# Casts moved into the DMA, fillers re-sized and casts spread in a fused sparse-attention and ELU-MLP kernel

## The chip, the cores and the metric

One core of one Trainium2 chip. The metric is the device time of one launch in microseconds (us). The kernel before takes 348.42 us, the median of three runs (348.39 to 350.0). All runs use one core, so a run counts as slow when it is over 1.5% above the fastest of the same kernel, and ratios use the other runs only.

## The reference, cut to what matters

```python
# q, k, v: (8 batches, 8 heads, 576, 64) float32
scores = (1/8) * q @ k.T
mask_local   = (rel >= 0) & (rel < 32)                    # heads 0 to 3
mask_strided = (rel >= 0) & (pos_k % 32 == pos_q % 32)    # heads 4 to 7
attn = softmax(where(mask, scores, -1e9)) @ v
x = attn.transpose(0, 2, 1, 3).reshape(4608, 512)
h = x @ w_in                                              # 512 -> 2048
g = where(h > 0, h, exp(min(h, 0)) - 1)
out = g @ w_out                                           # 2048 -> 512, float32
```

The matmuls run in bf16. Attention of one batch feeds 576 tokens to the two MLP layers, which are most of the work.

## The kernel before

Attention of batch 0 runs alone at the start (0 to 31 us). Layer one of its tokens follows, then batch 1 between pieces of layer two, and from about 75 us a loop mixes attention of batches 2 to 7 with the MLP. In the profiles PE is TensorE and PEld its weight loads, DVE is VectorE, ACT is ScalarE, POOL is GpSimd and SP is SyncE. `hpw` and `hps` are results of layer one (four and two blocks wide), `ops` of layer two, `g` is the ELU's output, and `so`, or `s_ps` and `o_ps`, are the sums and products that a tail takes up. A load lands when its data has arrived. In the program's names a piece `T` transposes q and k on TensorE, `S` makes scores, exp and the masked product `pm`, `M` multiplies by ones and v, `E` is the tail (ln, exp, product into `xT`), `X` is `M` and `E` together, `f` and a digit are filler matmuls that keep TensorE's clock up, and `2` is a quarter of a layer-two tile. In the list of batch 0, `c` is the second k cast, `m` the strided mask and `v` the v casts. Pieces are numbered by head pair and half: 0 to 3 are local, 4 to 7 strided.

The parts that the argument touches, cut (`# ...`):

```python
w_in_sb = const([128, KC, d_ff], BF16, "w_in_sb")        # one tile, two loads into it
for i in range(2):
    nc.gpsimd.dma_start(out=w_in_sb[:, :, i * 1024:(i + 1) * 1024],
                        in_=w_in_v[:, :, i * 1024:(i + 1) * 1024])
# ...
def cast_q(eng, a): ...      # ql32 (float32) -> qlb (bf16), on a chosen engine
def cast_k(eng, a): ...      # kl32 -> klb
def cast_v(eng, b, a): ...   # vl32 -> vlx[b % 2]
# ... batch 0
for it in ("f4 S0 S1 c f4 T1 m S2 f4 T2 S3 f4 S4 T3 f4 S5 f4 S6 M4 f2 S7 f2 E4 M5 f2 E5 M6 f2 E6 "
           "v M7 f2 E7 M0 f2 E0 M1 f2 E1 M2 f2 E2 M3 f8 E3").split():
    n = int(it[1]) if len(it) > 1 else 0                 # one digit only
    # ...
# ... batch 1, beside layer two of batch 0
for it in ("2 S4 2 S5 2 2 X4 2 S6 X5 2 S7 2 X6 2 X7 v "
           "a 2 2 T0 2 S0 S1 2 T1 B0 2 S2 B1 E0 2 S3 E1 B2 2 B3 E2 2 t E3 x").split():
    # "a" casts q on DVE, k on ACT and GpSimd, v on GpSimd;
    # "t" transposes the strided heads of batch 2; "B" is M in another buffer
    # ...
# ... layer two, at the end of a tile
if part == 3:
    nc.scalar.copy(o_sb, ops)                            # ACT; traced as osb<-ops
    store(j * SUB + kk * 128, o_sb)
# ... in the loop
def casts2():                # batch 2: k, q, k, q and then v, v, all on GpSimd
    ...
at(2, casts2)
```

The softmax here doesn't subtract the row's maximum and nothing guards it: scores larger than these inputs give would overflow.

## Time and profile before

| view | number |
|---|---|
| median of three runs | 348.42 us |
| the profiled run | 350.58 us, span 348.9 us, mean granted clock 0.966 |
| TensorE (PE) busy | 93% of the span |
| fillers in the trace | 74: 26 ahead of all, 48 in batch 0 |
| first layer-one group that runs in full | at 30.61 us |

The profiled run was 2 us longer than the median, and its clock lower than in most runs (0.966; the median of 96 later runs of this kernel is 0.980). A difference of two traces therefore overstates the gain by about 2 us, and what follows says where that matters.

The summary of the chain of waits, by engine, from the page of the kernel before:

```profile
PE 68%; ACT 12%; DVE 11%; DMA 4%; issue 3%; SPq 1%; ACTq 0%; DVEq 0%
```

TensorE is two thirds of it and DMA only 4%. The start of layer one in the timeline of PE. Columns: start and length in us, engine, line of the kernel, operation, what it writes from what, sizes, count; in brackets the idle time before and what ended it:

```profile
30.61 1.80 PE L393 MATMUL hpw<-xT,w_in_sb 128*128 128x256 bf16 x15 [0.26 <-DVE xT L282]
32.25 1.91 PE L367 MATMUL hps<-xT,w_in_sb 128*128 128x256 bf16 x16
```

Layer one waits for `xT`, the attention output of batch 0, for 0.26 us. The line says nothing of the weights, which had landed by then. By the trace of the loads the two halves of `w_in` were issued at 6.9 and 7.7 us and took 17.0 and 21.8 us, so the second landed at 29.5, only 1.1 us before.

### The profile page before, as it was taken

The page shows a single profiled execution, that of the slowest core. Times are in us where ns is not written, and L with a number is a line of the kernel's source. Part 1 is how long each engine was busy: PE and PEld are TensorE (multiplying, and loading weights), DVE is VectorE, ACT ScalarE, POOL GpSimd, SP SyncE. Part 2 cuts the span into 40 slices and gives each one's busy share as a digit, 9 for nine tenths or more (in the row PEclk, how much of TensorE's full clock was granted, in tenths as well). Part 3 has the DMA queues.
Part 4 walks back from the last instruction along what each step waited for, and adds up shares of the span by engine and source line. Part 5 has one row for each costly group of instructions (what it writes and reads, how often), then busy time and mean ns, then how long its engine had stood idle before and what let it go on. Part 6 is the DMA issues. An engine that isn't in the chain of part 4 may idle for free.

```text
span 348.9 us, 7582 instructions
## 1 busy us (share of the span) xinstructions
PE 323.0 (93%) x2926; PEld 222.9 (64%) x2926; DVE 247.1 (71%) x479; ACT 221.0 (63%) x426; POOL 109.2 (31%) x125
## 2 busy tenths in 40 slices
PE   7799898776989999999899999999999999999995
PEld 5557864354656666677566766666777766777762
DVE  4532994457767788889887897789888776766660
ACT  3466757654667777777677766777777776444441
POOL 8076712656257242615306351635000000000000
PEclk9658999996999999999999999999999999999999
DMA  8999998988649982999159975994193101111111
GB/s 161 187 201 204 218 165 134 202 159 178 111 86 139 197 176 56 135 195 203 41 85 133 210 172 103 169 216 114 30 150 72 38 24 34 49 30 32 43 49 60
DMA packets 49739, 43.26 MB, mean 124 GB/s; under 512 B 32808, under 2 KB 39720, under 8 KB 49704
## 3 DMA queue, kind: packets, MB, share of 16 engines
q0 software_dynamic: 15600, 25.77, 42.9%
q1 hardware_dynamic: 32780, 16.42, 23.6%
q10 hardware_dynamic: 1324, 0.59, 0.9%
q8 instruction: 23, 0.38, 0.5%
q14 instruction: 12, 0.10, 0.1%
HBM read 38.21 MB, written 9.44 MB: 137 GB/s over the span
## 4 chain that ended last, share of the span: by engine, by line
PE 68%; ACT 12%; DVE 11%; DMA 4%; issue 3%; SPq 1%; ACTq 0%; DVEq 0%
PE ops L426 28%; PE hps L367 27%; PE sc L258 4%; DVE he L382 3%; ACT he L375 3%; DVE g L383 2%; DMA kl<-in_k_dram 2%; ACT osb L431 2%; PE idle L436 2%; DMA ksT<-ks 2%; PE ox L310 1%; ACT ln L314 1%; ACT ln L313 1%; PE tp L233 1%; PE hpw L393 1%
## 5 line engine op out<-in xcount | busy, mean ns | idle before, releaser
L426 PE MATMUL ops<-w_out_sb,g 128*128 128x512 bf16 x576 | 146.9, 380 | 3.6 <-ACT osb L431 3.6
L367 PE MATMUL hps<-xT,w_in_sb 128*128 128x256 bf16 x1088 | 143.1, 275 | 2.3 <-DVE xT L282 1.4
L367 PEld LDWEIGHTS <-w_in_sb 128*128 128x128 bf16 x1088 | 116.1, 114 | 22.4 <-issue 2.8
L375 ACT ACTIVATE he<-hps 128x512 f32<-128x512 f32 x136 | 80.7, 595 | 64.1 <-PE hps L367 62.8
L383 DVE TENSOR_TENSOR g<-he,hps 128x512 bf16<-128x512 bf16 x130 | 89.4, 688 | 14.3 <-PE hps L367 1.0
L382 DVE TENSOR_SCALAR he<-he 128x512 bf16<-128x512 f32 x130 | 63.4, 488 | 25.2 <-ACT he L375 24.2
L426 PEld LDWEIGHTS <-g 128*128 128x128 bf16 x576 | 52.0, 98 | 44.5 <-issue 5.3
L261 ACT ACTIVATE e<-sc 128x576 bf16<-128x576 f32 (+1 forms) x64 | 41.0, 647 | 18.7 <-PE sc L258 18.6
L431 ACT COPY osb<-ops 128x512 f32<-128x512 f32 x36 | 21.0, 583 | 10.4 <-PE ops L426 9.3
L282 DVE TENSOR_TENSOR xT<-ox,rc 64x288 bf16<-64x288 f32 x40 | 18.2, 454 | 7.1 <-ACT rc L316 6.3
L278 DVE TENSOR_TENSOR xT<-ox,rc 64x288 bf16<-64x288 f32 x40 | 18.1, 454 | 6.3 <-ACT rc L316 5.7
L111 POOL DMA_DIRECT2D qs<-in_q_dram x8 | 6.5, 816 | 44.8 <-DMA qsT<-qs 33.8
L269 DVE TENSOR_TENSOR pm<-e,mask_l 128x576 bf16<-128x576 bf16 x32 | 15.5, 496 | 6.7 <-ACT e L261 6.5
L313 ACT ACTIVATE ln<-ox 64x288 f32<-64x288 f32 x40 | 16.3, 408 | 5.8 <-PE ox L310 4.9
L263 DVE TENSOR_TENSOR pm<-e,mask_s 72x576 bf16<-72x576 bf16 x32 | 15.9, 513 | 4.9 <-ACT e L261 4.9
L316 ACT ACTIVATE rc<-ln 128x288 f32<-128x288 f32 x40 | 17.8, 444 | 1.3
L132 POOL COPY vsx<-vs 72x1024 bf16<-72x1024 bf16 x10 | 10.7, 1095 | 25.0 <-DMA vs<-in_v_dram 25.0
L436 PE MATMUL idle<-warm 128*128 128x256 bf16 x74 | 16.1, 367 | 1.3 <-DVE warm L155 1.3
L126 POOL CAST vlx<-vl 128x768 bf16<-128x768 f32 x15 | 13.0, 890 | 12.5 <-DMA vl<-in_v_dram 11.5
L120 POOL CAST klb<-kl 96x768 bf16<-96x768 f32 x13 | 11.5, 884 | 16.0 <-DMA kl<-in_k_dram 10.0
L314 ACT ACTIVATE ln<-ox 64x288 f32<-64x288 f32 x40 | 16.1, 403 | 0.5
L117 POOL CAST qlb<-ql 72x1024 bf16<-72x1024 f32 x12 | 12.9, 1076 | 7.2 <-DMA ql<-in_q_dram 7.2
(86 smaller groups left out, 266.4 us busy)
## 6 DMA issues: line engine op xcount, KB each, us to landing
vl<-in_v_dram POOLq DMA_DIRECT2D x8, 576.0 KB, 17.2
out_dram<-osb SPq DMA_DIRECT2D x32, 144.0 KB
kl<-in_k_dram POOLq DMA_DIRECT2D x7, 576.0 KB, 14.1
ql<-in_q_dram POOLq DMA_DIRECT2D x7, 576.0 KB, 15.2
qs<-in_q_dram POOLq DMA_DIRECT2D x8, 288.0 KB, 6.7
ks<-in_k_dram POOLq DMA_DIRECT2D x8, 288.0 KB, 9.1
vs<-in_v_dram POOLq DMA_DIRECT2D x8, 288.0 KB, 10.4
w_in_sb<-in_moe_w_in_dram POOLq DMA_DIRECT2D x2, 1024.0 KB, 19.4
```

Of the source, the lines that this page charges most:

```text
L261: nc.scalar.activation(e[0:R], sc[0:R, :, 0:W], ACT.Exp, scale=scale)
L278: nc.vector.tensor_mul(xs[:, u * W:(u + 1) * W], o[pr], rc[pr])
L282: nc.vector.tensor_mul(dst, o[pr].rearrange(pat, b=3, s=NS), rc[pr].rearrange(pat, b=3, s=NS))
L313: nc.scalar.activation(ln[lo], o[0][hi], ACT.Ln)
L314: nc.scalar.activation(ln[hi], o[1][lo], ACT.Ln)
L367: nc.tensor.matmul(hps[:, mm], lhsT=w_in_sb[:, c, (m // 4) * 512:(m // 4 + 1) * 512].rearrange("c (p mm) -> c mm p", mm=4)[:, m % 4], rhs= ...
L375: nc.scalar.activation(e, hps, ACT.Exp)
L382: eng.tensor_scalar(e1, e, scalar1=1.0, scalar2=1.0, op0=ALU.min, op1=ALU.subtract)
L383: nc.vector.tensor_tensor(gt, e1, hps, op=ALU.max)
L426: nc.tensor.matmul(ops, lhsT=g[:, m, kk * 128:(kk + 1) * 128], rhs=w_out_sb[:, m, :], start=(m == 0), stop=(m == MC - 1))
L431: nc.scalar.copy(o_sb, ops)
L436: nc.tensor.matmul(ps, lhsT=warm[:, 0:128], rhs=warm[:, 0:ps.shape[-1]], start=True, stop=True, skip_group_check=True)
```

## The change

Its intent: take casts off the engines in the stretches where TensorE has holes. In the compute part the kernel after lies 25 lines further down, so L367, L382 and L393 become L392, L407 and L418. In its list of batch 0, `X3` is not `M` and `E` but `T3` with a wider PSUM buffer. The core of the diff, cut:

```diff
+    def load_ql16(b):   # cast in the DMA, straight into the tile that is read
+        nc.gpsimd.dma_start(out=qld[0:RS], in_=q[b, 0:HG].rearrange(...))
+    def load_kl16(b): ...      # one per head, into klb
+    def load_vl16(b): ...      # two per head, into vlx
@@ transposes of local q, batches 1 and 2: two halves of 64 columns each
+                if type(x) is list:
+                    for z in range(2):
+                        nc.tensor.transpose(o[z * D:(z + 1) * D], x[z], identity[0:n, 0:n])
@@ batch 0
+    cast_k(nc.vector, 1)                    # was on ACT
-    for it in ("f4 S0 S1 c f4 T1 m S2 f4 T2 S3 f4 S4 T3 f4 S5 f4 S6 M4 f2 S7 f2 E4 M5 f2 E5 M6 f2 E6 "
-               "v M7 f2 E7 M0 f2 E0 M1 f2 E1 M2 f2 E2 M3 f8 E3").split():
+    for it in ("f7 S0 S1 f6 T1 f6 S2 S3 m f10 T2 f6 S4 S5 f3 X3 f3 S6 f3 S7 M4 f3 E4 M5 f3 E5 M6 f3 E6 "
+               "v M7 f3 E7 M0 f3 E0 M1 f3 E1 M2 f3 E2 M3 f10 E3").split():
         n = int(it[1]) if len(it) > 1 else 0
@@ batch 1
+    nc.gpsimd.memset(qlb[64:RP], 0.0)       # was behind the loads
     load_kl(1, nc.gpsimd)
-    load_ql(1, nc.gpsimd)
+    load_ql16(1)
     load_vl(1, nc.gpsimd)
-    nc.gpsimd.memset(qlb[64:RP], 0.0)
     # ... four memsets of vlx and vsx stay here, one small one joins them
     load_str(2, ks, k)
+    load_vl16(2)
-               "a 2 2 T0 2 S0 S1 2 T1 B0 2 S2 B1 E0 2 S3 E1 B2 2 B3 E2 2 t E3 x").split():
+               "a 2 T0 2 S0 S1 2 T1 k B0 2 E0 S2 2 B1 S3 E1 2 B2 E2 2 B3 t 2 E3 x").split():
-            cast_q(nc.vector, 0)
-            cast_q(nc.vector, 1)
+        elif it == "k":
+            load_kl16(2); load_ql16(2); load_kl(3, ...); load_ql(3, ...); load_vl(3, ...)
@@ loop
-    at(2, casts2)
-        ld, sp, ca, tr = (9, 3, 4, 3) if b == 3 else (9, 6, 5, 3)
+        ld, sp, ca, tr = (9, 3, 5, 3) if b == 3 else (9, 6, 5, 3)
-        at(st - ca, lambda b=b: casts(b))
+        for i, f in enumerate(casts(b)):    # order k, k, q, q, v, v
+            at(st - ca + .5 * i, f)
```

More of the change, by code (lines that the diff above doesn't have):

```diff
@@ L76 @@
     qlb = const([RP, 2, NS, 2 * D], BF16, "qlb")
+    qld = qlb.rearrange("p a s c -> p (a s c)").rearrange("p (h c) -> p h c", h=HG)
     klb = const([LQ, 2, LB, 2 * D], BF16, "klb")
@@ L108, in load_vl, with load_kl16, load_vl16 @@
         eng.dma_start(out=t[0:PRE, 1:], in_=x[LQ - PRE:, 0:HG * LB - 1, :])
+    def load_ql16(b):
+        nc.gpsimd.dma_start(out=qld[0:RS], in_=q[b, 0:HG].rearrange("h (p s) d -> p h (s d)", s=NS))
+    def load_kl16(b):
+        for h in range(HG):
+            nc.gpsimd.dma_start(
+                out=klb[:, h // 2, :, (h % 2) * D:(h % 2 + 1) * D],
+                in_=k[b, h].rearrange("(t p) d -> p t d", p=LQ))
+    def load_vl16(b):
+        for h in range(HG):
+            x = v[b, h].rearrange("(t p) d -> p t d", p=LQ)
+            t = vlx[b % 2][:, h // 2, :, 2 * (h % 2) * D:(2 * (h % 2) + 1) * D]
+            nc.gpsimd.dma_start(out=t[PRE:128], in_=x)
+            nc.gpsimd.dma_start(out=t[0:PRE, 1:], in_=x[LQ - PRE:, 0:LB - 1, :])
     def load_str(b, dst, src):
@@ L213, in t_parts @@
             dst = qlT[i][:, a * 8 * n:(a + 1) * 8 * n]
-            blk = [qlb[0:n, a, j] for j in range(NS)]
+            blk = ([qlb[0:n, a, j] for j in range(NS)] if b not in (1, 2) else
+                   [[qld[0:n, 2 * a + x, j * D:(j + 1) * D] for x in range(2)]
+                    for j in range(NS)])
         else:
@@ L232, in piece_T @@
             for j, x in enumerate(blk):
-                nc.tensor.transpose(ps[i][:, j * n:(j + 1) * n], x, identity[0:n, 0:n])
+                o = ps[i][:, j * n:(j + 1) * n]
+                if type(x) is list:
+                    for z in range(2):
+                        nc.tensor.transpose(o[z * D:(z + 1) * D], x[z], identity[0:n, 0:n])
+                else:
+                    nc.tensor.transpose(o, x, identity[0:n, 0:n])
         for i, (dst, blk) in enumerate(both):
@@ L471 @@
     cast_q(nc.vector, 1)
+    cast_k(nc.vector, 1)
     P = [(p, u) for p in range(4) for u in range(2)]
-    for it in ("f4 S0 S1 c f4 T1 m S2 f4 T2 S3 f4 S4 T3 f4 S5 f4 S6 M4 f2 S7 f2 E4 M5 f2 E5 M6 f2 E6 "
-               "v M7 f2 E7 M0 f2 E0 M1 f2 E1 M2 f2 E2 M3 f8 E3").split():
+    for it in ("f7 S0 S1 f6 T1 f6 S2 S3 m f10 T2 f6 S4 S5 f3 X3 f3 S6 f3 S7 M4 f3 E4 M5 f3 E5 M6 f3 E6 "
+               "v M7 f3 E7 M0 f3 E0 M1 f3 E1 M2 f3 E2 M3 f10 E3").split():
         n = int(it[1]) if len(it) > 1 else 0
-        if it == "c":
-            cast_k(nc.scalar, 1)
-        elif it == "m":
+        if it == "m":
             mask_strided()
@@ L484 @@
             cast_v(nc.gpsimd, 0, 1)
-        elif it[0] == "T":
-            piece_T(0, n, None, False)
+        elif it[0] in "TX":
+            piece_T(0, n, (nc.vector, nc.scalar if n > 1 else nc.vector), it[0] == "X")
         elif it[0] == "S":
@@ L494, in casts @@
     def casts(b):
-        for a in range(2):
-            cast_k(nc.gpsimd, a)
-            cast_q(nc.gpsimd, a)
-        for a in range(2):
-            cast_v(nc.gpsimd, b, a)
+        return ([lambda a=a: cast_k(nc.gpsimd, a) for a in range(2)]
+                + [lambda a=a: cast_q(nc.gpsimd, a) for a in range(2)]
+                + [lambda a=a: cast_v(nc.gpsimd, b, a) for a in range(2)])
     def spreads(b):
@@ L524 @@
             nc.gpsimd.memset(t.rearrange("p a t (y d) -> p (a t) y d", d=D)[:, :, 1, :], 1.0)
+    nc.gpsimd.memset(vlx[0][0:PRE, :, 0].rearrange("p a (y d) -> p a y d", d=D)[:, :, 0:3:2, :], 0.0)
     for h in range(2):
@@ L559 @@
             cast_k(nc.scalar, 0)
-            cast_q(nc.vector, 0)
             cast_k(nc.gpsimd, 1)
-            cast_q(nc.vector, 1)
-            load_kl(2, nc.gpsimd)
-            load_ql(2, nc.gpsimd)
             for a in range(2):
                 cast_v(nc.gpsimd, 1, a)
-            load_vl(2, nc.gpsimd)
+        elif it == "k":
+            load_kl16(2)
+            load_ql16(2)
+            load_kl(3, nc.gpsimd)
+            load_ql(3, nc.gpsimd)
+            load_vl(3, nc.gpsimd)
         elif it == "t":
@@ L594 @@
         at(n, lambda p=p: do(("TT", 2, p)))
-    def casts2():
-        for a in range(2):
-            cast_k(nc.gpsimd, a)
-            cast_q(nc.gpsimd, a)
-        load_kl(3, nc.gpsimd)
-        load_ql(3, nc.gpsimd)
-        for a in range(2):
-            cast_v(nc.gpsimd, 2, a)
-        load_vl(3, nc.gpsimd)
-    at(2, casts2)
     for b in range(3, B):
         st = int(SC[b][0])
-        ld, sp, ca, tr = (9, 3, 4, 3) if b == 3 else (9, 6, 5, 3)
+        ld, sp, ca, tr = (9, 3, 5, 3) if b == 3 else (9, 6, 5, 3)
         if b > 3:
```

## The prediction

> **What bounds the kernel now.** I read the page first, for where the engines are not full.
>
> ```profile
> PE   7799898776989999999899999999999999999995
> PEclk9658999996999999999999999999999999999999
> DMA  8999998988649982999159975994193101111111
> ```
>
> One digit is a fortieth of 348.9 us, 8.7 us. From the eleventh slice on (87 us) PE reads 9 or 10 tenths at full clock, so there the kernel is bound by TensorE and a change of copies and casts can win little. The holes are before: the granted clock is down in slices 2 to 4 and 10, and PE is at 7 to 8 tenths in slices 8 to 10. The diff works in just these stretches, with one exception (the casts from batch 3 on).
>
> Next I cut the first 94 us at the moments at which the clock record changes (5.03 us, then every 3.41 us) and asked for busy time by engine. Columns: busy PE, PEld, DVE, ACT, POOL, each with its count, granted clock, DMA share, GB/s.
>
> ```profile
> 8.44:11.86 3.42, 1.27 (x20) 0.95 (x18) 1.92 (x6) 1.97 (x3) 0.45 (x1) 1.00 1.33 190
> 11.86:15.27 3.41, 3.40 (x36) 2.41 (x36) 1.86 (x6) 1.30 (x2) 0.00 (x0) 0.50 1.13 196
> 25.51:28.92 3.41, 3.41 (x32) 1.70 (x31) 1.37 (x3) 2.77 (x7) 2.83 (x5) 0.50 1.20 190
> 66.47:69.88 3.41, 1.90 (x24) 0.92 (x23) 1.37 (x3) 2.21 (x6) 0.19 (x1) 1.00 0.99 219
> 76.71:80.12 3.41, 1.35 (x24) 1.13 (x25) 3.14 (x2) 2.28 (x5) 3.41 (x5) 1.00 0.89 136
> 80.12:83.54 3.42, 1.79 (x16) 1.38 (x16) 3.21 (x6) 0.86 (x2) 2.83 (x4) 0.50 0.78 170
> 83.54:86.95 3.41, 3.41 (x34) 1.99 (x34) 1.80 (x4) 2.02 (x5) 1.37 (x2) 0.50 0.89 204
> ```
>
> Two windows with PE busy 1.27 and 1.35 us (37 and 40%) are each followed by half clock; one with 1.90 us (56%) is not. After the first drop the clock stays at half for 17 us, until 28.92, although PE counts as fully busy. The chain of waits runs through PE in that time, fillers included (0.54 us for two, 0.96 for four), so batch 0 there goes at the pace of half-speed matmuls.
>
> Then the timelines of DVE, POOL and PE at the second hole.
>
> ```profile
> 76.98 2.23 DVE L379 SCALAR_TENSOR_TENSOR g<-he,he 128x512 bf16<-128x512 f32 x1 [2.13 <-ACT he L378]
> 79.13 1.04 DVE L382 TENSOR_SCALAR he<-he 128x512 bf16<-128x512 f32 x1
> 80.88 1.81 DVE L263 TENSOR_TENSOR pm<-e,mask_s 72x576 bf16<-72x576 bf16 x2
> ...
> 76.85 0.83 POOL L120 CAST klb<-kl 96x768 bf16<-96x768 f32 x1
> 77.62 1.03 POOL L117 CAST qlb<-ql 72x1024 bf16<-72x1024 f32 x1
> 80.54 1.84 POOL L126 CAST vlx<-vl 128x768 bf16<-128x768 f32 x2
> ...
> 81.75 0.45 PE L333 MATMUL so<-pm,ones 72*64 72x288 bf16 x2 [3.69 <-DVE pm L263]
> ```
>
> The same L379 operation takes 0.69 us at 85.43 and 91.62; beside POOL's casts of batch 2 it takes 2.23 and ends at 79.21, after the cast that ends at 78.65. Everything behind it on DVE is late, PE waits 3.69 us, its clock falls, and the next two hps groups take 1.83 us each in place of 0.87.
>
> Last, batch 1, where the chain of waits has a cast in it:
>
> ```profile
> 58.96 0.34 issue
> 59.30 0.97 DVE qlb L117
> 60.27 0.05 issue
> 60.32 0.70 PE tp L233 x14
> ```
>
> **What the Trainium skill says.** "TensorE: Matmul & The Clock Gate", Part 1, says that the clock is half or full, set by how busy PE was in windows of 3413 ns that do not start with the kernel. This trace agrees: its changes lie 6.83, 17.07, 51.20 and 6.83 us apart, multiples of 3.41. "SBUF — State Buffer", section "SBUF: two separate sides", says that DVE and GpSimd share one port pair as an exclusive lock for whole instructions, taken by DVE in two-port modes, or with two SBUF inputs against a reading GpSimd operation. The 2.23 us above fits. "DMA: Bandwidth & Descriptors", section "SWDGE vs HWDGE vs iDMA", says that a cast in a DMA is issued from GpSimd only, with descriptors computed there; so the diff adds POOL issue time. The trace has it: a load of one strided operand, which casts already, costs 0.70 to 0.76 us of POOL.
>
> **The change, part by part.**
>
> *Batch 0 (0 to 30.6 us).* Fillers go from 48 to 75, second k cast from ACT to DVE, T2 and X3 copied by two engines. The k data lands at 9.98 in both. DVE casts it (q's 1024 columns took 0.64 us, so 768 take about 0.5) by 10.5, then does two pm (1.0) and two copies (0.8): S2 at 12.35 against 11.88 now. In the window to 11.86 PE then has two groups of six fillers and the transposes of T1, about 1.95 us busy, close to the 1.90 that kept the clock. I take it that it stays full. Going on with 0.65 us per exp, 0.46 per pm, 0.45 and 0.64 for DVE's and ACT's copy: S4 at about 15.4 (15.47 now), S5 right behind (17.75 now), S6 at 18.4 (19.07), S7 at 19.3 (20.59). From there ACT is the limit: eight ln and rc pairs at 0.85 plus the v cast 0.81, from 20.15, is 27.8, and xT at 28.2 against 30.57. Gain 2.3 us. Moving the 2.0 us qlb memset off 35.8 takes perhaps 0.3 off DVE's L1 work (an L382 beside it took 1.32 in place of 0.42).
>
> *Batch 1 (58.9 to 74.9).* The two q casts on DVE (0.97 and 0.58) go. T0 now waits for ACT's k cast at 59.61, so it ends at 59.95 instead of 61.0: 1.0 us. Half-width transposes add eight matmuls per T, about 0.03 us each, 0.25. The new order lets E0 run before S2, and E3 beside the transposes of batch 2: step by step I get S2 1.5 us earlier and the first hps of the loop at 71.0, a gain of 3.9 if nothing else holds it. POOL does. The new v load of batch 2 is eight issues queued ahead of POOL's k and v casts of batch 1, and issues wait for old landings:
>
> ```profile
> 33.13 1.20 POOL L107 DMA_DIRECT2D vl<-in_v_dram  x1 [0.78 <-DMA ks<-in_k_dram]
> 35.09 0.74 POOL L108 DMA_DIRECT2D vl<-in_v_dram  x1 [0.76 <-DMA w_out_sb<-in_moe_w_out_dram]
> ```
>
> Each waits for the transfer eight issues before it. By that count the eighth v issue waits for ks of batch 2, landed at 58.6 (issue 46.52 plus 12.1), and the vs issue behind for the first v piece, perhaps 59.7. DMA share is near 1 until 60 us, so these times don't move up with the rest. POOL's k cast then ends near 61.3, where the moved-up chain wants it at 60.2, and v comes 0.6 later still: I take off 1.4. Net 2.5.
>
> *Batch 2 (74.9 to 92).* POOL's casts go: two of k and two of q (3.5 us), two of v (1.84). DVE's row from 76.98 becomes 0.69, then 0.42 and 0.69 and two pm at 0.41: the first "so" starts at 79.15 in the present frame, not 81.75. At full clock ACT leads: exp and relu of the next tile 1.0, two tails 0.86 each, he 0.5, two exp 1.1, he 0.5; the "so" now at 89.03 comes at 84.2. Gain 4.8.
>
> *Rest.* Two T of batch 2 get 0.25 each. From batch 3 on POOL does the same casts in another order; its queue is in order and the casts wait for data, not for their place in the program, so "spread" moves little. For batch 3 one q cast goes behind the second T, which makes POOL's run from 99.70 about 1 us longer beside DVE: minus 0.3.
>
> Sum: 2.3 + 0.3 + 2.5 + 4.8 - 0.5 - 0.3 = 9.1 us, so 348.4 - 9.1 = 339.3. It should stay to the end, as PE is full after 93 us at the same amount of work.
>
> **The rivals.** (1) The clock still drops at 11.86. For: 1.95 us is an estimate beside a limit that the trace only puts between 1.35 and 1.90. Against: fillers are denser, so it should come back sooner than at 28.9. Batch 0 then gains 0, or loses a microsecond: about 341.5. (2) POOL, held by the queue of issues, takes the whole gain of batches 0 and 1. For: the landings above and DMA near its limit. Against: batch 1's q and k land by 51.5, before use. Kept: 4.8 and 1 us or so, about 343. (3) POOL is never held, as the eight-issue count is read off two waits only: all of 3.9 comes, and about 338. (4) DMA pieces half as wide at the destination (128 bytes, not 256) land late and batch 2's transposes wait: against it is that they are asked for at about 62 and needed near 85, while loads took 7 to 10 us here.
>
> **Range and chances.** The third part is the surest, as two traced waits vanish with their cause; 3.5 to 5.5. Batches 0 and 1 together give 5.1, with 1 to 7 possible. Most of the doubt pulls down. I say 339.3 us, 335.5 to 343.2 eight times in ten. Two per cent faster is 341.45: chance 0.75; within 2% 0.23; slower 0.02.
>
> **What would show it.** Right: granted clock full from 5 us through the first 100; first hpw matmul at 28.3; no wait of 3 us at the first strided "so" of the loop; L379 never above 0.8 us there; hps of the loop beginning near 70 and the "so" now at 89.0 near 79.5. Wrong: half clock in slices 2 to 4, a POOL wait on landings at 47 to 60 us that T1 or B0 waits for by more than 2 us, or a new PE wait between 90 and 110 us which gives the gain back.

## The result, and the profile after

| | before | after |
|---|---|---|
| median of three runs, us | 348.42 (348.39 to 350.0) | 345.17 (345.08 to 345.22) |
| the profiled run, us | 350.58 | 345.22 |
| span in the trace, us | 348.9 | 343.4 |
| mean granted clock of that run | 0.966 | 0.990 |
| ratio of fast runs | | 0.989 (0.985 to 0.993) |

A ratio here and below is the mean time of one kernel's fast runs over that of the other's of the same rounds, so it is not quite the ratio of the medians quoted. In brackets behind it stands its 95% interval. The change gave 3.3 us by the medians, 1.1%; 9.1 us had been predicted. The result lies outside the range that was given.

The page of the kernel after, at the rows that the prediction showed of the kernel before:

```profile
PE   8686998877999999999999999999999999999995
PEclk9998999989999999999999999999999999999999
...
PE 65%; ACT 11%; DMA 10%; DVE 8%; issue 3%; POOL 2%; SPq 0%; ACTq 0%; DVEq 0%
PE ops L451 30%; PE hps L392 27%; DMA w_in_sb<-in_moe_w_in_dram 6%; PE sc L283 3%; ACT osb L456 3%; ACT he L400 2%; DVE g L408 2%; DVE he L407 2%; DMA out_dram<-osb 2%; ACT ln L339 2%; ACT ln L338 2%; PE ox L335 1%; DMA ksT<-ks 1%; DVE g L428 1%; PE tp L258 1%
```

The clock is nearly full (full was predicted), and DVE's share of the chain fell from 11 to 8%. New is a DMA: the load of the first layer's weights is 6% of the chain, and PE has a 6 in the fourth slice (26 to 34 us). PE's timeline there:

```profile
26.14 0.27 PE L418 MATMUL hpw<-xT,w_in_sb 128*128 128x256 bf16 x1
29.57 2.82 PE L418 MATMUL hpw<-xT,w_in_sb 128*128 128x256 bf16 x15 [3.15 <-DMA w_in_sb<-in_moe_w_in_dram]
32.19 2.62 PE L392 MATMUL hps<-xT,w_in_sb 128*128 128x256 bf16 x16
```

The last part of `xT`, DVE's timeline before and after:

```profile
30.10 0.46 DVE L282 TENSOR_TENSOR xT<-o_ps,rc 128x288 bf16<-128x288 f32 x1 [0.62 <-ACT rc L352]
...
26.92 0.46 DVE L307 TENSOR_TENSOR xT<-o_ps,rc 128x288 bf16<-128x288 f32 x1 [0.35 <-ACT rc L377]
```

It is done at 27.38 us instead of 30.56, which is 3.2 us earlier. Layer one does not follow: its second matmul, which reads this part, waits for the weights until 29.5 (so 2.2 of the 3.15 us are theirs alone), and then the 15 matmuls take 2.82 us instead of 1.80. The windows of the clock record say why, and show a second place of the same kind. Columns: stretch, its length, then busy PE, PEld, DVE, ACT, POOL with counts, granted clock, DMA share, GB/s:

```profile
26.86:30.28 3.42, 0.71 (x7) 0.70 (x8) 0.46 (x1) 0.03 (x1) 3.42 (x5) 0.99 1.15 189
30.28:33.69 3.41, 3.41 (x19) 2.37 (x17) 0.00 (x0) 1.26 (x2) 2.26 (x3) 0.51 1.12 214
71.22:74.64 3.42, 1.58 (x18) 0.95 (x15) 1.83 (x5) 1.34 (x3) 1.49 (x2) 0.99 1.08 205
74.64:78.05 3.41, 3.41 (x31) 2.23 (x30) 0.69 (x1) 1.60 (x4) 0.00 (x0) 0.51 1.01 163
```

A window with PE busy 0.71 of 3.42 us is followed by half clock, and one with 1.58 too. So the wait for the weights costs twice: once as idle time, once in the speed of what follows. DVE's first product of layer one shows what is left of the 3.2 us. Before:

```profile
34.42 1.23 DVE L403 SCALAR_TENSOR_TENSOR g<-we,wr 128x1024 bf16<-128x1024 f32 x1 [3.86 <-ACT wr L402]
```

After, with the third operation behind it:

```profile
34.40 1.22 DVE L428 SCALAR_TENSOR_TENSOR g<-we,wr 128x1024 bf16<-128x1024 f32 x1 [7.03 <-ACT wr L427]
...
36.67 2.37 DVE L407 TENSOR_SCALAR he<-he 128x512 bf16<-128x512 f32 x1
```

34.40 against 34.42: nothing is left. And the operation at 36.67 takes 2.37 us, where the same one took 1.32 before and takes 0.42 undisturbed. Beside it GpSimd (POOL) does four memsets back to back, from 36.45 to 39.9.

The second hole. ACT's timeline after, ahead of the loop:

```profile
72.43 0.58 ACT L456 COPY osb<-ops 128x512 f32<-128x512 f32 x1 [2.51 <-PE ops L451]
72.91 0.42 ACT L375 ACTIVATE ln<-s_ps 128x288 f32<-128x288 f32 x1
```

PE's timeline in the same place, with the first two `so` that wait:

```profile
74.34 3.15 PE L392 MATMUL hps<-xT,w_in_sb 128*128 128x256 bf16 x15 [1.84 <-DVE xT L307]
...
79.80 0.31 PE L358 MATMUL so<-pm,ones 72*64 72x288 bf16 x2 [0.72 <-DVE pm L288]
...
85.29 0.31 PE L358 MATMUL so<-pm,ones 72*64 72x288 bf16 x2 [0.30 <-DVE pm L288]
```

The same before, on ACT and on PE (the first `so` there, at 81.75, stands in the prediction):

```profile
72.41 0.59 ACT L431 COPY osb<-ops 128x512 f32<-128x512 f32 x1 [1.47 <-PE ops L426]
...
74.90 1.80 PE L367 MATMUL hps<-xT,w_in_sb 128*128 128x256 bf16 x15 [1.38 <-DVE xT L282]
...
89.03 0.31 PE L333 MATMUL so<-pm,ones 72*64 72x288 bf16 x2 [0.83 <-DVE pm L263]
```

The wait of 3.69 us that the prediction showed at the first strided `so` is now 0.72 us, so batch 2's casts did what was hoped. But the loop starts with a wait of 1.84 us for `xT`. ACT had been idle for 2.51 us, and then ran the copy of a layer-two tile first and the ln of the last tail (E3) behind it, though the sums for that ln were ready at 70.2. Half clock follows in this trace, so 15 matmuls take 3.15 us instead of 1.80.

### The profile page after: what moved, and what is told of

It is laid out like the page before. It is cut to its first block, busy times and chain, and to the rows that moved or that the text cites. A ratio compares the mean times of both kernels' runs of the same rounds, so it can differ in the third digit from the quotient of the medians.

```text
span 343.4 us, 7671 instructions
## 1 busy us (share of the span) xinstructions
PE 320.0 (93%) x2967; PEld 221.7 (65%) x2967; DVE 241.6 (70%) x476; ACT 220.9 (64%) x427; POOL 110.3 (32%) x129
## 4 chain that ended last, share of the span: by engine, by line
PE 65%; ACT 11%; DMA 10%; DVE 8%; issue 3%; POOL 2%; SPq 0%; ACTq 0%; DVEq 0%
PE ops L451 30%; PE hps L392 27%; DMA w_in_sb<-in_moe_w_in_dram 6%; PE sc L283 3%; ACT osb L456 3%; ACT he L400 2%; DVE g L408 2%; DVE he L407 2%; DMA out_dram<-osb 2%; ACT ln L339 2%; ACT ln L338 2%; PE ox L335 1%; DMA ksT<-ks 1%; DVE g L428 1%; PE tp L258 1%
## 5 line engine op out<-in xcount | busy, mean ns | idle before, releaser
L392 PE MATMUL hps<-xT,w_in_sb 128*128 128x256 bf16 x1088 | 143.4, 276 | 2.5 <-DVE xT L307 1.8
L392 PEld LDWEIGHTS <-w_in_sb 128*128 128x128 bf16 x1088 | 116.5, 114 | 23.1 <-issue 2.9
L407 DVE TENSOR_SCALAR he<-he 128x512 bf16<-128x512 f32 x130 | 63.1, 485 | 24.4 <-ACT he L400 23.3
L288 DVE TENSOR_TENSOR pm<-e,mask_s 72x576 bf16<-72x576 bf16 x32 | 15.2, 492 | 4.2 <-ACT e L286 4.1
L294 DVE TENSOR_TENSOR pm<-e,mask_l 128x576 bf16<-128x576 bf16 x32 | 14.7, 473 | 3.7 <-ACT e L286 3.4
L138 POOL CAST klb<-kl 96x768 bf16<-96x768 f32 x11 | 10.7, 994 | 18.1 <-DMA kl<-in_k_dram 10.7
L144 POOL CAST vlx<-vl 128x768 bf16<-128x768 f32 x13 | 11.2, 889 | 16.1 <-DMA vl<-in_v_dram 13.6
L461 PE MATMUL idle<-warm 128*128 128x256 bf16 x83 | 14.4, 315 | 1.3 <-DVE warm L173 1.3
L283 PEld LDWEIGHTS <-ksT 64*128 64x128 bf16 x256 | 5.9, 98 | 11.8 <-issue 7.7
```

Of the source, the lines that this page charges most:

```text
L392: nc.tensor.matmul(hps[:, mm], lhsT=w_in_sb[:, c, (m // 4) * 512:(m // 4 + 1) * 512].rearrange("c (p mm) -> c mm p", mm=4)[:, m % 4], rhs= ...
L407: eng.tensor_scalar(e1, e, scalar1=1.0, scalar2=1.0, op0=ALU.min, op1=ALU.subtract)
```

## The experiments

Fifteen kernels ran, in four batches, each on a chip of its own with the kernel before beside them. The theories at the start, by the letters that the expectations use where they name them:

- A, the weights: layer one of batch 0 waits for the second `w_in` load, so that all that batch 0 gains is lost there. A rival was the clock alone: half clock at 30 us costs the gain, whatever causes it.
- C, the order: the tail E3 stands behind the copy of the layer-two tile in ACT's order and starts the loop late.
- E, the spread: the casts of batch 3 and later, in their new places and order, take away stalls of DVE at 161 to 171 us, a gain that the prediction did not count.
- F, the queue: GpSimd's issues that wait for landings cause the scatter of the variant with batch 2's part alone. It came up after the first call.

An expectation that names another theory says in its own text which one it is. First all kernels and results; the readings follow one by one. "Before" is the median of the kernel before in the same call.

| label | kernel | runs | median us | before us | ratio (95%) |
|---|---|---|---|---|---|
| split | changed, `w_in` in two tiles | 6 | 342.74 | 349.00 | 0.983 (0.978 to 0.987) |
| warm | changed, 36 fillers ahead of layer one | 10 | 345.02 | 349.00 | 0.987 (0.983 to 0.992) |
| b0only | before, with batch 0's part | 22 | 349.23 | 349.00 | 1.001 (0.998 to 1.003) |
| b2only | before, with batch 2's part | 22 | 349.21 | 349.00 | 0.991 (0.987 to 0.994), 13 slow |
| again | changed, once more | 6 | 343.92 | 347.82 | 0.986 (0.981 to 0.991) |
| e3first | changed, E3 ahead of a layer-two piece | 5 | 340.65 | 347.82 | 0.978 (0.974 to 0.982) |
| msearly | changed, GpSimd's memsets at the start | 6 | 344.39 | 347.82 | 0.988 (0.983 to 0.994) |
| best1 | split, counts read in full, e3first, memsets early, v late | 5 | 342.77 | 347.82 | 0.984 (0.980 to 0.989) |
| nospread | changed, casts in their old places | 6 | 344.41 | 348.60 | 0.987 (0.983 to 0.992) |
| parse | changed, counts read in full | 6 | 342.26 | 348.60 | 0.983 (0.978 to 0.987) |
| split_e3 | split and e3first | 6 | 339.84 | 348.60 | 0.977 (0.973 to 0.981) |
| best4 | split_e3 and parse, memsets later | 6 | 340.96 | 348.60 | 0.978 (0.974 to 0.982) |
| b2late | b2only with v loaded later | 22 | 348.26 | 348.97 | 0.994 (0.991 to 0.996), 7 slow |
| best5 | split, parse, e3first, v late | 6 | 339.34 | 348.97 | 0.972 (0.969 to 0.976) |
| nob0 | changed, batch 0 as before | 4 | 342.11 | 348.97 | 0.981 (0.977 to 0.985) |

All gave correct results. One caution on reading them: runs of one kernel scatter by 1 to 2%, and the scatter goes with the mean granted clock. Of 96 runs of the kernel before in these four calls, the 32 with a clock below 0.972 have a median of 350.5 us, the 24 at 0.985 and above one of 348.1. So one trace of a kernel is one draw, and where two traces are compared below, their clocks have been looked at.

### split: the weights in two tiles

```diff
-    w_in_sb = const([128, KC, d_ff], BF16, "w_in_sb")
+    w_in_h = [const([128, KC, 1024], BF16, f"w_in_h{i}") for i in range(2)]
-        nc.gpsimd.dma_start(out=w_in_sb[:, :, i * 1024:(i + 1) * 1024],
+        nc.gpsimd.dma_start(out=w_in_h[i],
@@ in l1 and l1_wide, for instance
-                    lhsT=w_in_sb[:, c, t * 256:t * 256 + 512].rearrange(
+                    lhsT=w_in_h[t // 4][:, c, 0:512].rearrange(
```

> The changed kernel with w_in in two tiles of 1024 columns, one DMA each, so that the first layer-one groups depend on the first DMA alone. Theory A: in the changed kernel the second hpw matmul waited, until 29.57 us, for the second w_in DMA, which it does not read (the column ranges of one tile, taken as address ranges from first to last byte, overlap from the second row block on); the first DMA has landed near 24 us. Then hpw runs from about 27.4 us (last xT of batch 0), the clock does not fall at 30.3, DVE's first g starts at 31.2 to 31.6 in place of 34.40, and the time is 342 to 343.5 us against 345.2. Rival B: the first DMA itself lands only near 29.5, as DMA is full; then hpw still starts at 29.5 and the time stays at 345.2 within 0.3.

342.74 us. The wait for the weights is gone. PE's timeline of this variant:

```profile
30.56 1.80 PE L418 MATMUL hpw<-xT,w_in_h 128*128 128x256 bf16 x15 [1.02 <-DVE xT L307]
```

It waits for `xT`, as in the kernel before. The first group needs columns 0 to 511 only, which are in the first load. In one tile, the columns of the second load lie, row block by row block, between those of the first. Taken as one range of addresses, the second load therefore reaches over everything from row block 0's column 1024 on. That would be why the first matmul (row block 0) ran at once and the second did not, though the second also needs the part of `xT` done at 27.38. The range is my argument; that two tiles take the wait for the weights away is shown. That they make the kernel faster is not: 0.983 (0.978 to 0.987) here and 0.986 (0.981 to 0.991) for the changed kernel in "again" overlap.

The start itself, 30.56, is no earlier than before, because this execution had a clock drop of its own in batch 0. Its windows:

```profile
11.14:14.55 3.41, 2.04 (x38) 1.59 (x40) 2.08 (x7) 1.83 (x3) 0.00 (x0) 1.00 1.16 205
14.55:17.96 3.41, 2.96 (x38) 2.13 (x37) 1.37 (x3) 1.74 (x3) 0.00 (x0) 0.50 1.09 170
```

A window with PE busy 2.04 us dropped here, while the prediction had taken 1.90 as enough. Three unprofiled runs of split at a clock of 1.0 took 341.6, 341.9 and 342.3 us, its three others 343.2 to 344.9. So it seems to be decided run by run whether batch 0 keeps its clock; only the profiled run shows the place of the drop.

### warm: keep the clock up, and leave the wait

```diff
-        n = int(it[1]) if len(it) > 1 else 0
+        n = int(it[1:]) if len(it) > 1 else 0
-    "... S2 S3 m f10 T2 ... M3 f10 E3"
+    "... S2 S3 m f1 T2 ... M3 f36 E3"
```

> The changed kernel with 36 fillers ahead of the first layer-one matmul, where the trace shows one (the program reads only the first digit of a count, so f10 gave 1). It bridges PE's idle time to 29.57 without moving the wait. Theory A says the wait for w_in cost twice: 2.2 us of start, and half clock from 30.3 to 33.7, where 31 layer-one matmuls took about 1.6 us more. With the clock kept full, hpw still starts near 29.6, the first g of DVE starts near 33.4 instead of 34.40, and the time falls by 0.5 to 1.0 us to about 344.4. If the clock there does not matter because DVE sets the pace, no change: 345.2.

345.02 us, the same as the changed kernel within the intervals; a gain of 0.5 to 1.0 us could not be seen in them. In its profile the clock is 1.0 throughout, the fillers run for 4.1 us from 25.9 and layer one starts at 29.83 at full speed. Its first product on DVE comes at 33.75, 0.65 us ahead of the changed kernel's. So of the loss at layer one some 0.7 us is the clock. The other 2.5 are the wait, which fillers can't take away, and up to 0.5 of it the fillers themselves, as the second load landed at 29.3 (issued at 7.7, 21.6 us to landing). The rival, that the clock alone took the gain, falls.

### b0only: batch 0's part alone, on the kernel before

```diff
+    cast_k(nc.vector, 1)
-    for it in ("f4 S0 S1 c f4 T1 ...
+    for it in ("f7 S0 S1 f6 T1 ...        # and the copies by two engines
```

> The kernel before with batch 0's part of the change alone (its fillers and order, the second k cast on DVE, copies by two engines). Theory A: batch 0 ends about 3 us earlier, but hpw starts at 29.5 instead of 30.61, at half clock, so the gain is about nothing: 347.8 to 348.8 us. My prediction had 2.3 us for this part: 346.1.

349.23 us against 349.00 in 22 and 47 runs, ratio 1.001: worth nothing, as A says. The profile has A's wait (DVE's first product comes at 33.59, 0.8 us ahead of the trace of before, and the time shows no gain from it):

```profile
28.52 3.05 PE L393 MATMUL hpw<-xT,w_in_sb 128*128 128x256 bf16 x15 [2.08 <-DMA w_in_sb<-in_moe_w_in_dram]
```

### b2only: batch 2's part alone, on the kernel before

```diff
     load_str(2, ks, k)
+    load_vl16(2)
-            load_kl(2, nc.gpsimd)
-            load_ql(2, nc.gpsimd)
-            load_vl(2, nc.gpsimd)
+        elif it == "k":                   # in the old order, behind T1
+            load_kl16(2); load_ql16(2); load_kl(3, ...); load_ql(3, ...); load_vl(3, ...)
-    at(2, casts2)
```

> The kernel before with batch 2's part alone: its local q, k, v cast by the DMA, no POOL casts of batch 2, batch 3's local loads issued earlier; batch 0's list, batch 1's q cast and order, and batch 3's casts as before. Theory: this part carries nearly the whole gain. L379 takes 0.69 us, the first strided so comes at about 79.2 instead of 81.75, the clock doesn't fall at 80.1, the so now at 89.03 comes at 84.5 to 85.5, time 344 to 345.5 us. If instead the four parts share the gain evenly, 347 us or more.

A median of 349.21, 343.17 to 358.24, with 13 of 22 runs counted as slow. The ratio uses the nine others and flatters the kernel; by the median it gains nothing, a miss. The profiled run was a slow one (358.24). There GpSimd's k cast of batch 1 stood behind the v issues, and those behind landings; the cast began at 63.84, PE waited 2.60 us for it, and half clock followed from 64 to 77.7. That is the hold that the prediction had feared for the changed kernel (where the cast runs at 59.45 and PE waits 0.46 us, for ACT's half of the k cast instead). Since it is seen in one slow run, no difference of times is explained by it here.

### again: the changed kernel once more

No edit.

> The changed kernel once more, beside the variants of this call and on their chip, as in the first set the kernel before spread from 346.0 to 352.2 us. Expected ratio to the kernel before 0.989 to 0.993 (345 to 346 us). If the three tight runs of the first comparison were a lucky state of the clock, it comes nearer to 1.

343.92 us against 347.82, ratio 0.986 on another chip. By the ratios the gain is 1.1% there and 1.4% here, and the intervals overlap: between 3 and 5 us.

### e3first: the last tail ahead of a piece of layer two

```diff
-               "a 2 T0 2 S0 S1 2 T1 k B0 2 E0 S2 2 B1 S3 E1 2 B2 E2 2 B3 t 2 E3 x").split():
+               "a 2 T0 2 S0 S1 2 T1 k B0 2 E0 S2 2 B1 S3 E1 2 B2 E2 2 B3 E3 t 2 x").split():
```

> The changed kernel with the last tail of batch 1 (E3) issued ahead of the transposes of batch 2 and of the last layer-two group. Theory C: in the changed kernel its ln waits on ACT behind the copy of that layer-two group, which waits for PE until 72.43 us, so xT comes at 73.83, PE idles 1.84 us and its clock halves for 3.4 us, in which 15 hps take 3.15 us in place of 1.80. With E3 first, xT is done near 71.3, hps goes on without a wait at about 72.2 in the time scale of the changed kernel, no half clock at 74.6, the first strided so at about 76.5 to 77.5 instead of 79.80; time 2 to 3 us less than the changed kernel. Rival: DVE and ACT, not this wait, set the pace of the loop's start, and at most 0.7 us is gained.

340.65 us against 343.92 of "again" in the same call, 3.3 us less by the medians and 2.8 by the means, with no run of the one as slow as the fastest of the other (341.01, 341.44), by an edit that adds and removes no instruction. On ACT the ln now starts where its sums are ready, and the copy comes later:

```profile
68.73 0.41 ACT L375 ACTIVATE ln<-s_ps 128x288 f32<-128x288 f32 x1 [0.38 <-PE s_ps L364]
```

And on PE the loop begins without a wait:

```profile
70.66 1.91 PE L392 MATMUL hps<-xT,w_in_sb 128*128 128x256 bf16 x16
...
75.09 0.31 PE L358 MATMUL so<-pm,ones 72*64 72x288 bf16 x2 [1.16 <-DVE pm L288]
```

C is shown, and with A's wait still there (layer one waits 3.09 us for the weights in this trace). That the first `hps`, at 70.66, is close to the 71.0 of the prediction is luck: the transposes ahead of the edit's place already begin at 68.75 here and at 70.31 in the changed kernel's trace, so 1.6 us of the difference between these two traces are not the edit's.

### msearly: GpSimd's memsets at the start

```diff
+    # the memsets of vlx and vsx: here, behind the w_in loads
     nc.vector.memset(vl32[0:PRE, 0, 0, 0, :], 0.0)
@@ ahead of layer one
-    # the memsets of vlx and vsx
```

> The changed kernel with the five memsets of vlx and vsx on POOL moved from 36.4 to 40.2 us into POOL's idle time at 9 to 19 us. Theory D: the L407 tensor_scalar that took 2.37 us at 36.67, beside four memsets in a row, takes 0.42, and batch 0's and 1's DVE chain ends about 1.5 us sooner; at the end 0.8 to 1.5 us less than the changed kernel. The cost could be up to 0.9 us at DVE's k cast at 9.8. Rival: batch 1 is held by landings and POOL's issue queue anyway, so nothing is gained at the end.

344.39 us, no gain: a miss. The conflict moved along with the memsets. The copy that builds the local mask on DVE, 0.37 us otherwise, now lies beside five of them (8.44 to 11.95 us):

```profile
7.48 4.63 DVE L209 COPY mask_l<-base_l 128x576 bf16<-128x576 bf16 x1
```

PE waited 3.55 us for the q cast behind it, and the clock went to half in batch 0. So DVE waited through several memsets in a row and not for one: the copy ends at 12.11, 0.16 us behind the fifth. By the profile it began 0.96 us ahead of the first, so what held it until then is not shown.

### best1: everything at once, too early

The edits of split, e3first, msearly, `int(it[1:])`, and `load_vl16(2)` moved behind `load_ql16(2)`:

```diff
     load_str(2, ks, k)
-    load_vl16(2)
@@ in "k"
             load_ql16(2)
+            load_vl16(2)
```

> The changed kernel with everything that the theories ask for: w_in in two tiles, filler counts read in full (f10 is 10), E3 ahead of the transposes, the POOL memsets early, and batch 2's v load issued behind its q load so that POOL's casts of batch 1 don't queue behind it. If the causes are as I read them and add up: layer one from 27.4 us at full clock, the loop's first hps at 68 to 70 us instead of 74.34, time 337.5 to 340 us. If landings of batch 1's k, q and v (50 to 57 us) bind instead, 340 to 342.

342.77 us: a miss, above e3first. It has the same wait of DVE's mask copy (4.46 us), which holds batch 0 until layer one starts at 33.22 us. It says little of its other parts.

### nospread: the casts of batch 3 and later in their old places

```diff
-        for i, f in enumerate(casts(b)):
-            at(st - ca + .5 * i, f)
+        fs = casts(b)
+        for f in (fs[0], fs[2], fs[1], fs[3], fs[4], fs[5]):
+            at(st - ca, f)
```

> The changed kernel with the casts from batch 3 on as before: in one block and in the old order (k, q, k, q, v, v). Theory E: the kernel before loses at 161 to 171 us, where the tensor_scalar L382 took 1.06, 1.09 and 2.01 us beside POOL's casts of batch 5, and the changed kernel gains 1.6 us there (copies of layer two go from 4.1 to 5.8 us ahead); with the old order those stalls come back, and the time is 1 to 2 us over the changed kernel, ratio to before about 0.991. My prediction: POOL's queue is in order, so place and order move little, at most 0.3 us.

344.41 us, ratio 0.987, the same as the changed kernel's 0.986 and 0.989. E falls. The lead over the trace of before grows by 1.7 us at about 170 us in this variant as well, and in b0only, where the loop is as before. So that step belongs to the trace of before, which had stalls of 1.06, 1.09 and 2.01 us on DVE at 161 to 169 us, and not to the spread.

### parse: the counts read in full

```diff
-        n = int(it[1]) if len(it) > 1 else 0
+        n = int(it[1:]) if len(it) > 1 else 0
```

> The changed kernel with the filler counts read in full, so that f10 gives 10 and not 1, ahead of batch 0's third transposes and of its last tail. Theory A: the last tail's nine more fillers only use up time in which PE waits for w_in until 29.5 us; the clock may still fall at about 30 as PE then idles 2.2 us; the nine ahead of T2 are done before its data (13.3 us) comes. So 0 to 0.7 us less than the changed kernel, mostly through fewer executions at half clock.

342.26 us, ratio 0.983 against 0.987 of nospread in the same call and 0.986 of again. The list of the change asks for `f10` twice, and `int(it[1])` reads a 1: the trace after has one filler at 12.23 and one at 26.02, and 57 in batch 0 where the list reads as 75. Read in full, they come out 0.4 to 0.6% faster; the intervals overlap, so a gain is likely and not settled.

### split_e3: both waits taken away

The edits of split and of e3first.

> Both waits off at once: w_in in two tiles, and E3 ahead of the transposes. If the two add, 1.2 us under E3 first alone (0.978 of before): 0.974, about 339 us. If landings and POOL's issue queue hold batch 1 once layer one starts earlier, no more than E3 first alone.

339.84 us, ratio 0.977. Its profile had full clock throughout:

```profile
27.23 1.80 PE L418 MATMUL hpw<-xT,w_in_h 128*128 128x256 bf16 x15 [1.01 <-DVE xT L307]
...
69.38 1.91 PE L392 MATMUL hps<-xT,w_in_h 128*128 128x256 bf16 x16
```

Layer one starts 3.4 us before that of the kernel before, and the loop starts 5.5 us earlier. With E3 in its place already (0.978 in another call), two tiles for `w_in` add too little to be told apart from nothing.

### best4: the memsets where DVE is less busy

The edits of split_e3 and parse, and the memsets of vlx and vsx moved behind the loads of batch 3 in "k".

> As split_e3, with filler counts read in full and with POOL's memsets of vlx and vsx moved behind its last load of batch 3, where DVE runs no tensor_scalar (about 70 to 74 us; first read after 100 us). Moved to 9 us they made one DVE copy take 4.46 us and lost all; here L407 near 36 should take 0.42 in place of 2.37, so 1 to 1.5 us less than split_e3: ratio about 0.970, 337 to 338.5 us. If POOL's issue queue binds batch 1 (its k cast waits), the gain is gone by 60 us and it ends equal to split_e3.

340.96 us, ratio 0.978: a miss, no better than split_e3. DVE's operations at the start of layer one are back to 0.42 to 0.49 us, so the conflict is gone there. But the clock fell in batch 0 of its profile, and layer one started at 28.85. Whether the memsets alone are worth anything in the time stays open.

### b2late: batch 2's part alone, v loaded late

The edit of b2only with `load_vl16(2)` moved into "k".

> Batch 2's part alone on the kernel before, as in b2only, but with its v load issued behind its q load. Theory F: the spread of b2only (343 to 358 us) comes from POOL's k cast of batch 1 held behind v issues that wait for landings (PE waited 2.60 us for it, then half clock for 13.7 us). With the v load later this is gone: no wait of PE for POOL's klb at the second local transposes, no run over 350 us, and a median of 344 to 345.5 us, i.e. nearly the whole gain of the change. If the spread has another cause, it stays above 10 us.

348.26 against 348.97, and the spread stays (343.76 to 356.99, seven of 22 slow). F falls: no cast of k is held here. Another conflict is seen instead. On DVE:

```profile
56.93 3.08 DVE L134 CAST qlb<-ql 72x1024 bf16<-72x1024 f32 x2
```

And on PE behind it:

```profile
59.46 0.43 PE L257 MATMUL tp<-identity,qlb 72*128 72x72 bf16 x8 [2.14 <-DVE qlb L134]
```

The two q casts of batch 1 took 1.55 us before. Here one of them took 2.47 us, beside GpSimd's v casts (57.26 to 58.85). In the kernel before these ran at 62.59, behind issues of loads that batch 2's part moves away. In the full change DVE has no q cast of batch 1, so nothing is there to be held. In this trace the lead over the trace of before falls from 2.4 us at 57 us to -0.1 at 72.4, and then grows by 4.8 until 109 us: batch 2's part gives its gain in full, and the conflict ahead of it costs 2.5. So it seems to be worth its gain only together with batch 1's part; that is read from one trace. The scatter of b2only and b2late goes with the mean clock (0.957 to 0.995), but what drops it in one run and not in the next stays open.

### best5: the best version

The edits of split, parse, e3first and v late, and the memsets left alone.

> Both waits off (w_in in two tiles, E3 first), filler counts read in full, and the v load of batch 2 issued later. If POOL's issue queue holds batch 1 once the start is earlier, this beats split_e3 by 0.5 to 1.5 us: ratio about 0.973, 338 to 339.5 us. If not, equal to split_e3 (0.977) within 0.3%.

339.34 us against 348.97, ratio 0.972 (0.969 to 0.976), with a clock of 1.0 in five of six runs. It beats both kernels. That its median is the time that had been predicted for the change is chance, as it has four edits more.

### nob0: the change without batch 0's part

```diff
-    cast_k(nc.vector, 1)
-    for it in ("f7 S0 S1 f6 T1 ...
+    for it in ("f4 S0 S1 c f4 T1 ...      # batch 0 as before
```

> The changed kernel with batch 0 as before. Theory A: batch 0's part is worth nothing in the changed kernel, as layer one can't start before 29.5 us: ratio to the kernel before 0.986 within 0.4%, as the changed kernel. My prediction's 2.3 us would make it 0.993.

342.11 us, ratio 0.981, all four runs within 0.3 us. It is no slower than the changed kernel and rather faster, though the intervals of different calls overlap. In its profile `xT` of batch 0 is done at 27.3 us with the old list too, because the clock was at half only around 12 to 15 us in that run and not for 17 us, and then PE waits for the weights here as well:

```profile
28.68 1.83 PE L418 MATMUL hpw<-xT,w_in_sb 128*128 128x256 bf16 x15 [1.52 <-DMA w_in_sb<-in_moe_w_in_dram]
```

DVE's first product comes at 32.51 here, 1.9 us ahead of the trace of before. So the 30.6 us that the prediction took as batch 0's end is what one execution showed, not what the kernel always does. The mean clocks say the same: 0.966 over 348.9 us is 23.7 us at half clock (17.1 in batch 0 and 6.8 at 80 us), while the median of the 96 later runs of before, 0.980, is 14 us, and only 18 of them have 0.966 or less.

## Why the prediction was wrong

Its sum was 2.3 + 0.3 + 2.5 + 4.8 - 0.5 - 0.3. Of its signs of being right, two came true (L379 at 0.69 us, no wait of 3 us at the first strided `so`); full clock up to 100 us, `hpw` at 28.3 (29.57), `hps` near 70 (74.34) and the `so` of 89.0 near 79.5 (85.29) did not. Term by term, by the trace of the changed kernel unless another is named:

1. **Batch 0, +2.3: the step that failed.** The arithmetic up to `xT` was not the error: 28.2 had been predicted, 27.4 came. The prediction let layer one start when `xT` is done. It then waited for the second `w_in` load (29.5), and DVE's first product came at 34.40 instead of 34.42: the term is 0. b0only measured 1.001 for it. Its sign, the first `hpw` at 28.3, had left the weights out. The load could be read in the trace of the kernel before, with 1.1 us of room, and a gain of 2.3 was credited past it. A second fault stands beside it: the 17 us of half clock, which made the old list look bad, were one draw, and with that list batch 0 can end as early (27.3 us in nob0). How much of the missing 2.3 us is the wait and how much this draw stays open, as two tiles didn't bring a measurable gain. Two smaller faults: the fillers were counted as 75 where 57 run, and "close to 1.90" was taken as enough for the clock, which split's trace refutes (2.04, and it dropped).
2. **The memset, +0.3.** It came out as a loss. Moving one memset forward left the other four in a row beside DVE's work (2.37 us instead of 1.32), and the first `so` of batch 1 came at 52.18 instead of 51.62: -0.56 us.
3. **Batch 1, +2.5: a step that failed too.** PE was 0.56 us behind at 52 us, and at the end of the last layer-two piece and the transposes, the same work in both orders, it was 1.0 us ahead (PE came to the loop's first `hps` matmul, which can run early, at 72.23 instead of 73.25), a gain of 1.6. The failing words are "E3 beside the transposes": E3's ln stayed behind the copy of the layer-two tile in ACT's order, and that copy came at 72.43 as before (72.41), because the transposes now ran ahead of its matmuls. So PE waited 1.84 us instead of 1.38, and the first full `hps` was at 74.34 instead of 74.90. The part thus gave 1.1 us, where 3.9 had been said before the 1.4 for the queue; without PE's wait behind E3 it would be about 3.2 (an estimate from this trace: the group going on at 72.3). e3first took the wait away and gave about 3 us. The 1.4 us taken off for GpSimd's queue weren't lost: issues did wait for the transfer eight issues before (3.02 us at 53.20), but PE did not wait for GpSimd's cast.
4. **Batch 2, +4.8: right, within half a us.** The stalled DVE operation went from 2.23 to 0.69 us and the wait of 3.69 to 0.72. From 74.34 to the `so` at 85.29 (89.03 before) the lead grew by 3.2 us, and half clock behind E3's wait took 1.35 of it (3.15 us for 15 matmuls, not 1.80); without it this is 4.5. In again, parse, nospread and nob0, where the clock stayed full there, the lead grew by 4.3 us up to this `so`. Up to the second copy of the loop, at 109 us, it grew by 4.75 (5.33 from the layer-two copy at 72.4, less 0.58 ahead of the first full `hps`).
5. **The rest, -0.5 and -0.3.** "Spread moves little" was right (nospread). The two negative terms weren't measured apart; between that `so` and 109 us, where batch 3 was to cost 0.3, the lead grew by 0.4 in those four traces.

Some lines were misread without moving a term: PE reads 6 to 7 tenths in slices 8 to 10, not 7 to 8, and 8 in two slices behind the eleventh; "7 to 10 us" holds for the loads of `qs`, `ks` and `vs`, while those of `kl`, `ql` and `vl` took 14 to 17 by the page.

So by the traces two waits took most of the gain of batches 0 and 1, and the first of them was no rival in the prediction at all. In the times the second is shown (e3first). For the first they show that batch 0's part is worth nothing (b0only, nob0), not that two tiles bring its gain back: split and again, and split_e3 and e3first, can't be told apart. Of its rivals, the second came out nearest in time (about 343) for the wrong reason: GpSimd's queue. The kernel without the two waits runs in 339.84 us (split_e3), and with full fillers and v late in 339.34; the prediction had 339.3. The sizes of batches 1 and 2 were about right, that of batch 0 was not seen in any time, and what had been left out was what else a stage waits for once its first wait is gone. How the gain of 1.9% in nob0 divides between batches 1 and 2 isn't settled, as batch 2's part alone makes a conflict of its own.

## What to carry to other kernels

Before you credit an earlier end of one stage, list everything else that the next stage waits for, with the time at which each lands; what arrives just in time (here 1.1 us ahead) is the next bound, and idle time costs twice where the clock follows the load. Look at each in-order engine for work of no hurry ahead of work that the next stage waits for: exchanging the two cost nothing here and gave about 3 us. Count in the trace what a list of fillers asks for, and take the clock of one trace as one draw of several.

## What the Trainium skill lacked or had wrong

- "TensorE: Matmul & The Clock Gate", Part 1, says that the window is free-running and the ramp varies from run to run; the runs agree. It gives no share of busy time below which a window counts as idle. Here windows with PE busy 0.71, 1.58 and, with transposes and matmuls of 64 to 96 rows among them, 2.04 of 3.41 us (split) were followed by half clock, and windows with 1.90 and 2.04 us (before, 66.47 and 73.30) and with 1.56 (parse, 70.74) were not. So there is no single limit on busy time as this profile counts it. Its remark that the ramp costs less than 1% of a typical span is about the start of a kernel. The later drops cost a like amount here (350.5 us for runs of the kernel before with a clock below 0.972, 348.1 for those at 0.985 and above, 0.7%), which is large beside a change of 1%: with the same list of fillers batch 0 ended at 27.3 us in one trace and at 30.6 in another.
- "SBUF — State Buffer", section "SBUF: two separate sides", says that the shared port pair is held for a whole instruction. The runs show DVE held through several GpSimd instructions in a row, but not always: 4.63 us for a copy of 0.37 beside five memsets, 2.37 us for an operation of 0.42 beside four, and in the trace of before 1.32 us for such an operation, which ended 0.28 us behind the first memset while more followed.
- "DMA: Bandwidth & Descriptors" has nothing on an issue that waits for the landing of the transfer eight issues before it on the GpSimd queue. Waits of 0.78 and 0.76 us in the trace of before and of 3.02 us in that of the changed kernel fit this; whether the chip or the program's semaphores set it was not tried.
- No page tells that a matmul may wait for a load of columns that it doesn't read when both lie in one tile (3.15 us here, 2.2 of it after the rest of its data was there, and no such wait in two tiles). This is most likely the program's doing and not the chip's.
